# Twelve more homes for feed-forward tiles, output rows interleaved with tiles, and 159 instead of 153 key blocks on VectorE's exp

## Chip, core and metric

One core of one Trainium2 chip runs the kernel. The metric is the device time of one launch in microseconds (us). A change of 0.2% is about 1.4 us here.

## What is computed

The reference is a transformer block whose two branches run in parallel on the same normalised input, with B = 1, S = 2048 tokens, D = 512, 32 heads of 16, and a feed-forward width of F = 1792:

```python
xn = layernorm(x)
q, k, v = split_heads(xn @ wqkv)
p = softmax(q @ k.T / 4)
attn = (p @ v) @ wo
h = relu(xn @ W_gate) * (xn @ W_up)
return x + attn + h @ W_down
```

The softmax makes 32 x 2048 x 2048 exponentials, and they are what the kernel is built around.

## The kernel before

The queries are cut into four chunks of 512 (`c4`), the 32 heads into four groups of eight (`gg`), each in two halves (`ee`): 32 attention blocks in that order. A block runs over 16 key blocks of 128 keys (`kt`). One key block holds four scores tiles of 128 keys x 512 queries, one for each of four heads.

**TensorE works in two halves.** Nearly every matmul uses a 64x32 tile of the array, and four of them side by side make one *group*: 64 rows by 128 columns on 512 streamed columns. The upper and the lower 64 rows are two *halves* with a chain of groups each, and the two run side by side. `score` (L1289 and after), `pv_stream` and `mm_chain` all record such groups. A group is preceded by a load of its weights unless the half still holds them from the group before (`emit`, L389 to L396), which is how three value products over the same values can share one load.

**Two ways to take exp.** A usual key block is two *units*. A unit is two score groups (one on each half) into one of two double PSUM banks, then one ScalarE instruction of 128x1024 (L1365) that writes exp into `ring`, and later two value groups (`ring` by `v_aug`). As there are two such double banks, the scores of unit u+2 can't start before the exp of unit u has read its bank, and the exp of unit u+2 can't start before those scores are there. In a key block marked in `QUAD_AT`, `quad` does the work without ScalarE: four score groups into single banks, four VectorE instructions that turn each bank into 16-bit integers which are read as bf16 numbers (L1320), then two further patterns of the same integers shifted by constants, one by VectorE (L1339) and one by GpSimd in two pieces (L1335, digit 2 in the table), or otherwise divided. All three patterns go through the value product, so a marked key block has six value groups (24 matmuls of 64x32) where the two units of a usual one have two for the pair (8 matmuls); the scores take four groups either way.

**Background work.** Between the scores and value products TensorE also makes the feed-forward tiles (`glu`: 16 groups into two banks, then a VectorE copy L1016 and a VectorE product L1020 that leaves a 128x512 tile in `hT`), and the output rows (`out_rows`: 14 tiles by `W_down` and four attention outputs by `wo`, 36 groups into one bank, a VectorE addition L1069 and a store). Rows of a chunk can start only when its attention is done. `seq` lists tiles and rows in the order in which they are wanted: 14 tiles of a chunk (some made next to the same tile of the next chunk, so that one transfer of their weights from memory serves both), then that chunk's four rows; a loop below it gives each job its wanted unit. Finished tiles live in `hT`, 20 places (`NHS`, pool `P_h`).

**The order is written out.** The instruction order of all engines, with every bank and place, comes from the string `PLAN`, made beforehand by a planner that isn't in the file. `Graph.run` (L324) only decodes it and adds the waits; each engine then runs its queue strictly in that order. So a change of tables or of `seq` comes with another whole order. Names that the steps below use: `ring` (ScalarE's exp), `qd` (VectorE's), `v_aug` (values), `hT` and `xnT` (the normalised input, transposed, 4 x 2048 columns, which is dead once a chunk's last projection and tile have read it; at the end the last rows' residuals are kept in its first 1024 columns by `resid`).

Of the kernel before, what the change touches and what calls it, by code (L numbers as in the profile page):

```python
# [121 lines left out]
PLAN_OPS = 8248  # L122
PLAN = (
    "c-m!K1z;3M7v67n?{Wzd96~7)9Euky#fn1{v}hoK;8KbdcXx*Z#UWUc1S{?yij?ARg%p<nA>8f!Z)SJzHvEN<&E4+Ilka`+dvmFxr2dbKFK%6lf2^OxpPcvTGN*FSxG*2!#(Uzg@iI@fAXj{^<+x8@"
    "%6)Si-}BZZIh1?Wi;8boZof|$L0|XHm3{A9SJrLzy}8dF<9#T;*NnG~=Zyz+<6X!r<1XE12mQnqv4Rfy92EJAaiv>UfZpcj3mo26tqZQ$U$U%#_ciYGN&bQHBUf~J#l2=5&xoHaJB&+R@m)eUmxgY6"
    "1Mf<TVy*7=RX$=o=v_jrEyKoj@vvM?guuAZe1Kaql;**5!dTnG<bKeNI7+LmDA0wmjtHuEL0$U9ZE&$8Qryc8bEQY-YT!n=#1=+S<f4Xo@?W{UVg>|8pbR&RMXi6VU8KqKRjx=k#ie36ubayl(KlZZ"
    "Hkp@Zm}T5xJ)_w0XF*%xKB#iV=avr+x@m*ulCD_6H(%v;1K@*@uf*hc-3Kr$F6MW|ECM5~#yipxX1ho6K#?I4w=!QwxG%ZBoN;c4Gq+cx`6k)JEI2SPpBQc_9_EqpWxi+|cG5G(8XkzOFxxIx2)WG;"
    "v#>-|tRzVEh^;*em;WkE095*CSm<HqH|`M|cr09qT?N{VqVkBF%{%E!F2OyVSrjJo#C@^#5)-#ki(ELx!R42&{H1*&2Hxz52r$buahFFFHO%CC#9Q)JX4)?UB?Bn-@h~$EIv~rA8_Cs;WrYXK$Nit2"
    "M!^`XNhfIu!$pr-LS8yEID~)F1h<%6rs(#5!hPxRm9Y^lkGYG%5gr*R0~OLCGBU+!z=V64=^WYo$tfJMfyPTKzOG}v;bF$wOvcRc*~FY;Bv>(tiF*u~8(XJvKX15AfN<jhZuJo_&2ULV6kSIO6u07Z"
    "n^5&Yev|jYSj=N$RJvkR9J6dQw^K}4WnknQ2KJbTo4lwq%O)-%r<f?UuuDHk&%DjiSK&Se(yeb+R>Tduswg~lX?yeb(aF4Nkg+hqF8uHqwZ!ZoHmb)Pd?OPS5BUuDmX8s2!)cF~_zloVDiYqnivk~q"  # L130
    "nY1CwOy{3m@(zy-tptie8y<@zOv?m=nS1CyhNEu=B`7eOk-4-{f*<_M5>EDG7OrJlj3<qH<B}A0Uq6ShIT>w0_7VdV7WXDQb<H4KFK}%NhI8+iw?X?D-P<nA;$d8|bq!xzx2@%?Juea2d0J6Ycihz4"
    "iKpttb}qMXVl_42%G{@Q45=jhvlSWL=1(da;oV)g$rSi7X|g-_={ghMqMLJ*p}1~7rOW*c)nvS?_#*193-N&Jm2bY<vBgpM1wl8Rg-!aJs>hOTHhssvVvX}uy4D`TRBeJ=Dnik}C}X4+x2a?83x)z8"
    "P7M7D-$pVbhF-Mp(9NeUoO!Rm(9_&TEIgIe=U=4H*8F8n=~jp=p$ePY^|cgh5n-d%d3{m#82#JSWxiUqOr$1lsdSSV4fZs9w5f$mrt#t2l1_2~v;V<-Ua~WEtC}S<>(DK_7H`2Y3_dto2=#_e`(*Vt"
    "g9R+@W;o|D>5$AY83nqH+ATj!ijo4rE1_gF@^%OKB%gf8QYqHkoEu9rL-W|xonmNwAueE>v%JypMjKYVr8c%?2{)Cy)N9<j!4?E=hFLc`6E;RMR`D1WWsO<B25P)&-fH?P6*#ko0@_pi<kkdX=$0AY"
    "b-5+Vm{;o?c`)6VVKthH$2WqAMUB=5`+#hhw3ZGx!(`SvynFdD{aNE?a4o!<6(z;2ck1!(p?il87~_pKDf!TwTKRHY?HQuc1c<PXTbt^pKioTXnWmT_=C;>JnKGs*-f6>xf;lFcv!dN{GbE;9x6M>u"
    "tGxmi+^fa8t?L>ypru?bvh&uSabXVK-jem|O>Rzxu+2K$8f>l3FN?r5-n!Fl)?9I`7NeRin;X0Yo9|xdypb~dl5M=V+J(jQTxUwEcI)dZ+$){!Ga*kcp}qZ)f7yfok84w%BYZKC*;~J_!F>T9pD$Lg"
    "wKR=+qeb4{Dc*a8A$73TabdB#?_Tq~fZmp;6JjBm8p}iYu<YymJXI&NkD1(em|@|J+X7_G_r|e=PXlpp!?%=(#HU<JN3zp?4wWi>+}2KQ8>O0Xl~f(sUZ(aVEw7$1k1xLH;Kqe{xT0`h;%p~f+y@f="
    "#p_;p@l;sh|G&hSV$NGd7UwJG5s<F|7}p*}VZKms-w?tjWty|PhuKd*OpyhXdll~h=qn<#3DUrn>{8^QZP1{H!?fBMj-cq?QyE3E23c=Ev+<-S)iIUHH1ypZowzl}*=oWjam0RH`z&R)mpDwI*-m<l"
    "-F07|Ft;`PiA9;#$$+)7uNRn3de2=9BdmiRk7BV6Yy}`&q(#PxSMb=*&x}+UozfUkpjaJ1w?-jDoZ4;U)~S*uq%4Y&t;FXmw^OfTQ-I1BptV7t`zB_<CwadlFOM}``;H!TQ?!_AHAhZ!d{$sJG>=UO"
    "d1G(1JfA4^wjMd;d86r_>22g_Vaiy^I@dFhV5&6Ejjp4Z+@^aMF;t8<-d594yhLR-ck95_cb;iKjx_V)v%mzJUGsU*?d;;frr#{In(EdXI=L}cf7WRB=e`4Acp1*BBi%UrvQE+zZg1!O|IYQTpS{dx"  # L140
    "$|c2ys{fY|+}6kKyz0d?-RgE28MgEzPu+w6uRGfN0k;H!ZxG?BdGL$7?I$6yW7*dV?1#Dh3u@)c7oS1c(QXGk=cxuQ+j&6h-r^gM6#U;x*8FCdAKuy4dLFh;>zmGX?)#j=D_LNDBBJ|t@SUU^D|oNG"
    "M@eQ@eZ#68w``rwHXEfvi<LiPH*@+_yo0?-A76~WHm_}JMuA-z!_p~&aCK4lrdEM9=c{hTMrZa<ldK$CM^8M}NNqn`u~d7itaI<-d#ZGCdp^DL$d(S9+jf{4kHI>%GGj?J$jx(H&OFv==beibWBj$w"
    "78R@SS;vST>oWzj$$7kEnRwbf@3So{=Ky95OXf)@^Du9dvMExXS<|k0<X}IAlAVehW?Lud<{+jh7R`IfT(=$E8T`X+XIOfwdXXSEWS_y&1}vCIM1iOJ>_oTb3-hBKZYg`8#b$f-wtZ`&P<-0ME;qcN"
    "W?8gsJ#CF~)`xSjv$|!Ki4?1)n`5H)Lm1hi%mXT)q~c!=S2k+09pR?_e1xYyd9&$m`-j1)`nmT5Q!hmM7jusHsZ>W%itn>jbJnr5lwFbXR39v*5(Zx?Z`((whHU3H;p`pAQk}(k&-)al+T16Uzxcc&"
    "RfzZ(AKAh7nJ)KDNvYgVb!h87$m7PG<dye!D)1ho=wEzNXdB<`r}MtHl4=^TO)p;6<^2>uNeu~KRCV||_LpmkzZsDFzXwh@Kfi|x##s@lx~l4@OK6(^Csp@P!L#(5pL!pe@iZ&^#O;|ikDrJBIxmN5"
    "HyIw}rPmy8`iIeXaYL}@CCkXz)iBM;{=sc}|0W6mIT%9TF{GhwRDQm6LOGnKJ#hi`S>=^LuFA(Mvz@dGeWyQ22CA=YyP#~k7n$CqnbBT%{vHFAOSuPp9hmHNyRHGnpJhl1czXvZ@+yt?%5lBqEqc@K"
    "@_R-$`0WU;wk3kD(v2yNW0SWbxDXIBDo1;b7GB<w?bB-Q9d#?VO&GuTs1t4fJ`RoPZvgPB*F*%hUk^NU?IE`537o-SWpLtorXIj=Ps8zN+UJ=nlmRZTja;7+{Vi~5Y3r40x)<%XeXmzN98`{cN^-j0"
    "fu(`{F5Suacfe8S^3L<yulNl(wMc8P4gG2hurmG8JuJLbLm*xomQu&X;_m{dn{NBjHD;vVzeC}x6wC2>@8r@So!kn<J)Xg@6mqj))2D1m*$32$)E&z^YR$--<((F{UF=7%#r{*^W`WB^)n9=rxgPDQ"
    "F$@^z!spLh&jO=dZ*wFEJR1U(Y>?tmH#HqWacd6enr7=R0b|ywiw~4apw}i8|0^YJlC~U($=(JN-4uw6IC5O?5kC!R<Qj;_tJ^PH2Q(dosa@yM#i(sl`-DB99ZKc8l^^L6{ssoejoj}(hq;xHhVQ6^"
    "_5pg|S+BPP37FY?QgYyj1fXJ)BYg^Rfc%(<&jVNH1S(I%uS3T#j`HgrA#VMU2H#w!2$TX^6=9d%MP>qZS7G_}f_d(=7<26m(DGjP$!Okc4p1W4ec74QbrSd!{oSsj4VwVRdydASi3GN%(=P%CS<j0o"  # L150
    "qTL6w)EqZzLh0SQs^94KFA(XcPe$L*<VWkzepAqE7K&c}2FC}vV`HG6Am~QB%XaR1QsDYv?@RkPd<^>Ncj7jXv(%C@IFk`*=y)IU-v1AvKKx>v&Fn*oeTeSgM<OYN(9`)Ckl3u<!gZ}xk%K6#Vy#gU"
    "I1&1jn=L^UW&8*l)zuDGIZBsR9xyB!`rrEMp{s#r&*D(54m(AV>8qbYI$+wI?(-cnYbag$_xa&Tb2r(Mh;lKpQOjfIQSmve&VC$#`hSwjiNJwgJ5cBMN<iMFXup&%Kl%L-jQ<@d_z8Y*6AAG74x!Sm"
    "uL*G&F^+oEi2YR#CL$9D=Jv+qq2q^AEk6l-h#U`5n2O?7*0d=RJ0I+-yQgywAonsP^`ugKg3E1cj2+gZLqW=9w!GJztl_!Rny2R8gwsHUuP0-G`!3aI*um=Bvh5Q^S~t6!<HC*RC9@JVSsU(PwD@j("
    "p4)=6P-GbTC*70t$y20NHHuP~E{kIpclj6DAGf4<bSi<*UjhH&{PpCLDSkD9;aVrm?}o7Zi0g%{EjBh=*NVb_16iDp@UjqX@!wgOqUBdJ10$;3DEKyD;m?nFmfBQ~>|HBh9b**}7{a~*Hq6ooU}`_S"
    "Z$Z_Y2?v`#IpU(ro10o;Rg(>r-R(%xTMXj=u68THwj?KWJJDcUeQZwB)C{gFK+>Ojc6@f?M=G4MC%*MNx#caDTD$&J7hTozP|EK8MG$HdUnlS%;)Rq3o1BfdeD$bwe9jvM?jGanno|M@RON2gyaHuB"
    "eIkb@Y}|}Bt+AR#mdD|y1i`{crcznwI94O&kVb5B8)<h|z|pF2D+6=tr$Ov8igxAJXveA%ym0-m3g<pXlOH1*eB2!2^gmtv-QEfMsfwq1Q4A8wYbS^)#_N8qvIAv1()PCt^qYK@XL>gln3SUe)~8G-"
    "!(U=Ki$)C~YMs_t8&%*F@aPg&W$ZJ%M;_p8!r^5kU9PX`@d^R15|lsPk*gD5=%G~Y!pjU)QvdV;{;jpI>Or<;<}85Xe`}q);EjYGz>rQja)XNR^!y~3uB*EMfA&Kwtcc+?b3WME=2Losv3aLr5lwIX"
    "F!b4y(<4S_&)%6_x{e7IPnA6tPql=7wf6m0_C!T?Y`eIfkhkM$a5aL*mCg(3{caD&(Q88)5mRE-1GNs+fIqQE?MGTD5z)E#^j_d%zHw(lS0aZFY;i}|x@+!krTagpmbC({lLFS_2O#UZzs53GZ~xJw"
    "2UGr$;ef6c0}<5-<}QQBU4{gYEq0+*o`vZCp4_UHHWKSzb(@=ME%94d%r5YBGq4W}oXG)iT`7)D#9f0QW3FF{)?#DhZdCWqmY=A(^em048#3cXz5KvbN8yXbFY%05i1xPPZ1^6xL#JdEWDWD-(d*#o"
    "Fkp7_Q@t=c06+gZ2xAvv%REs^TXyW2<yr;IDCT~J%n^bZR%2R8cT{XEs+g!wSW+zvZ`Re~QNWI5?Ll_eUu7d>o7}w2L+Vlcob~fO=-r+Ip>uEE+`a(%mdMBn9T#ug;D@Wr>SJ4N!ogu2{Givz!5Oq("  # L160
    "ySIo>AvYtn;Fhas$(01ks_rFYwQWS#ZC!Y{>)Vk;lAl|x?24X4LU|*?=@z$NV|}Rb>%vvWi0X!xMnbV`NSZ3}{xWxs&6s|!beq_-h(9uV=JS7Z6Ov1}x$~yoFS98~#OC#av^6526Z=f5`R+`C=GStN"
    ">8GYeu5h%6yEU+6>re6Z<GVj}5Kew0Na9spdZ;PW*EfyZDGF^#WlzN=`6!bigT@Uigb;FS9LoPVxJ;8(mnu-0j^bp|pf`K+7QFs8g7IPn+*=Bbs_0K-da*Cj`08m<g|9CeGG>Sa$+X*wF8XqvzO$um"
    "m-=;cPsttb{0!zyUWMnqsZor(9X9wDbF@B3u-}Hof3#?ixP@KNb=>OhlSt!?bewF*V&Z^7NH@7Q1ta72MinsgS3Vsj<JRN)n|d!W0r-nGsLXTVQrKLeAHvtiKc+l5kJQ{(MTMSFM$dI=&?M-!NEETE"
    "{3vnmK;ifC8Sy_+wU(cP3Mc1KmT(^#W85c2&18r=Qgu3hCU-W5BFk_puWD_IqW4UMQsFkPyF_d5pXvD&^6pSI=v{xx#~H$jk|SB~rwlsr@%%<>_C<jxs@A4A)J8t7NBAz!JCYoao?+BTj3US<CSrKi"
    ">L5!Vt?iM-2-eS$lpM7@3(inN9wY^9SXY0f=wWS9^*+zu?&YQxK=(%4vgWIWJw5SkL&xSo&_u028%;tis6%D<hi)s6_d(}Ioq(GEcFH<(C;@y8Vw!AdLQ18j5;&`49kih}hj2F=pDB7T?b*H}nr-F>"
# [1252 lines left out]
```

## Time and profile before

| | us |
|---|---|
| median of the three runs | 685.31 |
| lowest and highest run | 685.06, 686.58 |
| span of the profiled execution, first to last instruction | 684.2 |

The page gives no device time of the profiled execution beside its span, so the 1.1 us between span and median is taken as what lies around the span. In the rows that follow, PE is TensorE's matmuls, PEld its weight loads, DVE VectorE, ACT ScalarE and POOL GpSimd; a "<-" after an idle time names who ended it. A row of the timeline merges instructions that follow each other: its first number is when the first one starts, its second how long until the last one ends, and x is their count.

### The profile page before, as it was taken

What the parts mean: (1) busy time and instruction counts of PE and PEld (TensorE: products, weight loads), DVE (VectorE), ACT (ScalarE), POOL (GpSimd) and SP (SyncE); (2) the same over time, 40 slices, a digit from 0 to 9 for tenths busy, and PEclk for the clock granted to TensorE, in tenths of its full rate; (3) what the DMA queues carried; (4) which work ended last, traced back from release to release, by engine and by line L of the source; (5) the groups of instructions that cost most, each with busy time, mean ns of one, the idle gap of its engine ahead of it and who ended that gap; (6) DMA issues with size and microseconds to landing.
All of it is one profiled execution on the core that took longest, in us unless ns stands there. A gap on an engine that the chain in (4) does not pass through costs nothing.

```text
span 684.2 us, 45020 instructions
## 1 busy us (share of the span) xinstructions
PE 675.6 (99%) x22262; PEld 345.9 (51%) x19654; DVE 598.5 (87%) x1012; ACT 666.8 (97%) x730; POOL 499.8 (73%) x507
## 2 busy tenths in 40 slices
...
DMA packets 55940, 35.86 MB, mean 52 GB/s; under 512 B 19336, under 2 KB 51784, under 8 KB 55752
## 3 DMA queue, kind: packets, MB, share of 16 engines
...
## 4 chain that ended last, share of the span: by engine, by line
PE 75%; ACT 18%; DVE 5%; issue 1%; DMA 0%; POOL 0%; ACTq 0%
PE ps L250 75%; ACT ring L1365 18%; DVE stats L726 1%; DVE qd L1320 1%; DVE xn_sb L739 1%; DVE v_aug L876 0%; DMA x_sb<-in_A_x_dram 0%; DVE qT L952 0%; DVE mv L727 0%; ACT xn_sb L1164 0%; DVE qd L1339 0%; DVE xnT L780 0%; POOL rstd L721 0%; DVE xnT L1075 0%; DVE kT L869 0%
## 5 line engine op out<-in xcount | busy, mean ns | idle before, releaser
L1365 ACT ACTIVATE ring<-ps 128x1024 bf16<-128x1024 f32 x718 | 660.4, 1141 | 2.9 <-PE ps L250 2.5
L1335 POOL TENSOR_TENSOR qd<-qd,ints 128x512 int32<-128x512 int32 x446 | 450.5, 1041 | 143.8 <-DVE qd L1339 73.2
L250 PE MATMUL ps<-qT,kT 64*32 64x512 bf16 x8192 | 448.7, 374 | 1.3 <-DVE qd L1320 0.4
L1320 DVE TENSOR_SCALAR qd<-ps 128x512 int16<-128x512 f32 x612 | 396.7, 685 | 51.9 <-PE ps L250 49.0
L250 PE MATMUL ps<-qd,v_aug 64*32 64x512 bf16 x3672 | 263.0, 375 | 1.1 <-issue 0.9
L250 PE MATMUL ps<-ring,v_aug 64*32 64x512 bf16 x2872 | 236.5, 374 | 0.1
L1300 PEld LDWEIGHTS <-kT 64*32 64x32 bf16 x7584 | 151.1, 92 | 126.6 <-issue 32.6
L1272 PEld LDWEIGHTS <-v_aug 64*32 64x32 bf16 x4544 | 108.7, 91 | 75.6 <-issue 20.4
L250 PE MATMUL ps<-xnT,wgs 64*32 64x512 bf16 x1792 | 137.6, 374 | 0.0
L250 PE MATMUL ps<-xnT,wus 64*32 64x512 bf16 x1792 | 136.4, 374 | 0.0
L250 PE MATMUL ps<-Wd,hT 64*32 64x512 bf16 x768 | 59.0, 375 | 0.0
L810 PEld LDWEIGHTS <-wgs 64*32 64x32 bf16 x1792 | 43.1, 91 | 31.5 <-issue 7.4
L810 PEld LDWEIGHTS <-wus 64*32 64x32 bf16 x1792 | 43.2, 91 | 29.8 <-issue 7.6
L1339 DVE TENSOR_SCALAR qd<-qd 128x2048 int16<-128x2048 int16 x83 | 56.1, 690 | 2.3 <-PE ps L250 2.2
L810 PEld LDWEIGHTS <-hT 64*32 64x32 bf16 x1792 | 40.2, 92 | 28.2 <-issue 4.2
L250 PE MATMUL ps<-Wv,hT 64*32 64x512 bf16 x512 | 45.7, 375 | 0.0
L250 PE MATMUL ps<-Wk,hT 64*32 64x512 bf16 x512 | 42.8, 375 | 0.4 <-DVE qd L1320 0.3
L1020 DVE SCALAR_TENSOR_TENSOR hT<-ps,up_sb 128x512 bf16<-128x512 f32 x56 | 38.4, 685 | 4.6 <-PE ps L250 4.2
L1016 DVE COPY up_sb<-ps 128x512 f32<-128x512 f32 x56 | 38.4, 685 | 3.1 <-PE ps L250 2.5
L250 PE MATMUL ps<-Wo_p,x_sb 64*32 64x512 bf16 x480 | 40.2, 374 | 0.6 <-issue 0.5
L250 PE MATMUL ps<-xnT,Wq 64*32 64x512 bf16 x480 | 36.2, 375 | 0.0
L250 PE MATMUL ps<-xnT,Wk 64*32 64x512 bf16 x480 | 35.0, 374 | 0.3 <-DVE xnT L780 0.3
...
## 6 DMA issues: line engine op xcount, KB each, us to landing
...
```

The costliest lines, as they stand in the source:

```text
L250: return e.add_instruction(mybir.InstMatmult(name=e.bass.get_next_instruction_name(), engine=mybir.EngineType.PE, ins=[e.lower_ap(x), e.lo ...
L726: G.op("DVE", 580, lambda e, m=m: e.bn_stats(stats[:, m, :], xs(m)), reads=[t_xm[m]], writes=[t_st], prio=pr, order=last_xn if m == 4 else ())
L739: G.op("DVE", 320, lambda e, m=m, t=t_n: e.tensor_scalar(xn_sb[:, t.slot, :], xs(m), mv[:, m, 0:1], rstd[:, m:m + 1], op0=ALU.subtract, op ...
L810: e.ldweights(w()[rows, 32 * j:32 * j + 32], tile_position=(rows.start, 32 * j))
L1016: G.op("DVE", 603, lambda e: e.tensor_copy(up_sb[:, tup.slot, :], bank_of(tu)), reads=[tu], writes=[tup], prio=-590)
L1020: G.op("DVE", 603, lambda e: e.scalar_tensor_tensor(out=hT[:, th.slot, :], in0=bank_of(tg), scalar=0.0, in1=up_sb[:, tup.slot, :], op0=ALU ...
L1272: e.ldweights(vs(j), tile_position=(64 * half, 32 * j))
L1300: e.ldweights(ks(m), tile_position=(64 * half, 32 * m))
L1320: G.op("DVE", 601, lambda e, j=j, tx=tx: e.tensor_scalar(qd[:, tq.slot, 512 * j:512 * j + 512], ps[:, BANK[tx.slot], :], IBIAS[3], 0.0, op ...
L1335: G.op("POOL", POOL_NS / POOL_PIECES + 60, lambda e, x=x, n=n, c=slice(i * m, i * m + m): e.tensor_tensor(x().bitcast(I32)[:, c], raw().bi ...
L1339: G.op("DVE", 600, lambda e, n=n, x=x: e.tensor_scalar(x(), raw(), float(SHIFTS[n + 1]), None, op0=ALU.add), reads=[ti, tq], writes=[t], p ...
L1365: exp_ops[u] = G.op("ACT", 904, lambda e, tr=tr, k0=k0: e.activation(ring[:, tr.slot, :, :], ps[:, 4 * k0:4 * k0 + 2, :], ACTF.Exp, scale= ...
```

## The change

It has three parts: the pool of finished tiles gets 12 places in `xnT` (four for each of the first three chunks, usable for tiles of later chunks), a chunk's four rows move behind `ROW_STEP` tiles each of the next chunk, and six more key blocks are marked in `QUAD_AT`, one in each of the attention blocks 10, 12, 18, 21, 26 and 28. `PLAN` is another string, with 8302 instead of 8248 entries.

```diff
+ROW_STEP = (0, 1, 2, 2)
...
-    "2...3..3..2..3..",
+    "2.2.3..3..2..3..",
...
-    "3...3..3..2..3..",
+    "3.2.3..3..2..3..",
...
-        P_h = Pool("h", NHS)
+        P_h = Pool("h", NHS + 12)
...
+        def h_of(t):
+            if t.slot < NHS:
+                return hT[:, t.slot, :]
+            a, dt = divmod(t.slot - NHS, 4)
+            return xnT[:, dt, 512 * a:512 * a + 512]
...
-            th = t_h[(c4, ft)] = Tile("h", P_h)
+            th = t_h[(c4, ft)] = Tile("h", P_h, list(range(NHS)) + [NHS + 4 * a + dt for a in range(c4) for dt in range(4)
+                                                               if c4 < NB - 1 or a == 2 or dt in TAIL_ACT])
...
-                out=hT[:, th.slot, :], in0=bank_of(tg), scalar=0.0, in1=up_sb[:, tup.slot, :], op0=ALU.max, op1=ALU.mult),
+                out=h_of(th), in0=bank_of(tg), scalar=0.0, in1=up_sb[:, tup.slot, :], op0=ALU.max, op1=ALU.mult),
...
-                    pairs.append(((lambda th=t_h[(c4, ft)]: hT[:, th.slot, 128 * i:128 * i + 128]), (lambda ft=ft: wd_of(ft))))
+                    pairs.append(((lambda th=t_h[(c4, ft)]: h_of(th)[:, 128 * i:128 * i + 128]), (lambda ft=ft: wd_of(ft))))
...
-                         reads=[t, txr], writes=[tr] + (t_xnT if i == 0 else []), prio=p1)
+                         reads=[t, txr], writes=[tr] + (t_xnT if i == 0 else []) + [Tile("res%d" % a, P_h, [NHS + 4 * a + i]) for a in range(2)], prio=p1)
+                resids.append(o)
...
-        seq = []
+        seq, behind = [], []
         for c4 in range(NB):
-            rows = []
+            rows, tiles = [], []
...
-                seq.append(ffn[ft])
+                tiles.append(ffn[ft])
                 if ft in shared[c4]:
-                    seq.append((0, GN, lambda s, c4=c4, ft=ft: glu(c4 + 1, ft, s), W_LEAD + 2))
-            seq += rows
+                    tiles.append((0, GN, lambda s, c4=c4, ft=ft: glu(c4 + 1, ft, s), W_LEAD + 2))
+            step = ROW_STEP[c4]
+            for n, row in enumerate(behind):
+                seq += tiles[n * step:n * step + step] + [row]
+            seq += tiles[len(behind) * step:]
+            behind = rows
+        seq += behind
...
+        for a in range(3):
+            guard = Tile("xnT")
+            guard.r.extend(o for o in t_xnT[a].w + t_xnT[a].r if o not in resids)
+            P_h.cur[NHS + 4 * a:NHS + 4 * a + 4] = [guard] * 4
```

More of the change, by code (lines that the diff above doesn't have):

```diff
@@ L77 @@
     "2...3..3..0..3..",
-    "2...3..3..2..3..",
+    "2.2.3..3..2..3..",
     "2...3..3..0..3..",
-    "2...3..3..2..3..",
+    "2.2.3..3..2..3..",
     "2...3..3..0..3..",
@@ L93 @@
     "2...3..3..0..3..",
-    "2...3..3..2..3..",
+    "2.2.3..3..2..3..",
     "2...3..3..0..3..",
-    "2...3..3..2..3..",
+    "2.2.3..3..2..3..",
     "2...3..3..0..3..",
@@ L119 @@
 NHS = 20
[L122 removed]
+PLAN_OPS = 8302
 PLAN = (
[L124 to L165, printed above, removed]
[L166 to L218 removed]
@@ new lines @@
+    "c-mcC2Ow4N`#;Y)_g<T_652zlv?Zj{l+r>;C244BP+HoQwx~!-qFpGFku;6=x3s6xP_!lPJ?H<9b1uJsxcA(1-t)fC_&m?^d7pD*nE(AJ;6Fh+!Y|S%{L}I+I&8_jr3c~-0=<TR>1pAACKQ<Zb1mMXKjxjdO#S`R"
+    "E##WGTK%d*!*K$d1pU3Iq6z9H>V*&*3dPW)`T;y6fWZI1fxx350be2KKoXmrWTYeVNkA8QGz5J_KjaXN<^dlGcpfxa{pviOnkR=0J-}k4bE06P8a!EBeTobf>Q^Vn<Q~ylJQ12)z%Sy`SUOR1A^^TdhZDI#5b8Cc"
+    "Isi|tK;$Q*#ij9mqV!aIvOGB?>jJ(^43E!{8|dA{c0@K18n{3Zqys7ih}a^AMAB1b$=q00EEIJL8bse1(cyw<2_RRb6{XWeYPF5YB0RMeh<BlnEM7~6uhBtt9_kfF2~-sP!c#O*U6Gz@De;Qb9t@UUTt!@o*pN=f"
@@ new lines @@
+    "tL-R?Cb?9agb^A*TLP<EWeN<sq-c4v1k0#EtuV0_))$|p4kLzCflwc1;wqvK$n<qGY8^71r9vRn5Fypl5_hmFR>g?s;RP}T-B2%^Mh#kx73T+PJAz^nTmrQuqlTCmVk*%?jEY)WAU>eNh|);zBZ$Q6k(=;8e2+>1"
+    "^un-Aee`4b#1N8#3j`HQk%uN=Yh`#8uax1%kY?1XR3406q^)E@bTc)K3Sk0Gf<KUnk+v$9c$OvW5!vxfJWGwK!Y;=XsK`|;A~iNO7%Mp%B-e;Az;=}UMc#RyuBrk??Je>FucS60F|3NF7a}W-Kc1+Lr2r9g3^th<"
+    "7-()B{w(&57<A+$i-%K*iHs_OE78b;O27v-3gUb!q8RER;#dqwbv|Hd&JjenQzfXHcs8;Mky79Z(9jtb^$VJj=uLznXF)6l$SS;AcL{BPJjB!}NP@w5B#ThYQO}WOh&seaEFO=>(I`@hp^kru7({hJ#fdtJ@kr7r"
@@ new lines @@
+    "HW?bjk%Wxz=OwG+NySy@irBC~6;dOWXpKhjJS&bvi<8>~>S}61sADNGuuX{VS%zYatbn6}r71xCOb_vNwHgB81pt4f83|8Sqe(48j8Z47QLq$ryzoy`ov#IT;gj;9<Y@S-5LhY)F%EVTQH+`lxkpUB47IgNbQ^I7"
+    "LsbS|gc5_1B#po`Qd3}`5VaU3N3P-|Kua$UK;jY+KjI2%SL1mYh9y%Fn-SquKtqLuCkC&WeMz9=+e9xAUy&?|wILZ!prI$alo*p|STTSpS_!V`Xp~O{o(3rvnYu<rOCd=kL~$e>s3@>`MyfsNtddO0NRa16xT#aT"
+    "nkexqP6{(}0qU~{#SK+PsON6zwOX5LKsRWL=6Oy!K`WwY$_A_o`9S!8m5CNNkrOlo2!5%Rt5Y5?h{#muVYHqgU8Z9gb%McvWGzCpRIJ2=Xqr>vkOlD`n$g6xsbVMwNJdrh>>nK!l8hzkSF92YrA90{rd|=L2QM*A"
```

152 lines of the change are left out of this document (97 added, 55 removed).

## The prediction

> **What bounds the kernel now.** I read the page's totals first, then ScalarE's timeline over the whole span, then TensorE's timeline in a dense spot, and last the order in which the groups stand in the two programs' TensorE queues.
>
> ```profile
> PE 675.6 (99%) x22262; PEld 345.9 (51%) x19654; DVE 598.5 (87%) x1012; ACT 666.8 (97%) x730; POOL 499.8 (73%) x507
> ```
>
> Two engines are nearly full. TensorE's 99% is a modelled share, so it has to be weighed otherwise. ScalarE's timeline is firmer:
>
> ```profile
> 10.91 2.87 ACT L1365 ACTIVATE ring<-ps 128x1024 bf16<-128x1024 f32 x3
> 14.10 146.19 ACT L1365 ACTIVATE ring<-ps 128x1024 bf16<-128x1024 f32 x159 [0.32 <-PE ps L250]
> 160.47 2.85 ACT L1365 ACTIVATE ring<-ps 128x1024 bf16<-128x1024 f32 x3 [0.17 <-PE ps L250]
> 163.63 22.10 ACT L1365 ACTIVATE ring<-ps 128x1024 bf16<-128x1024 f32 x24 [0.31 <-PE ps L250]
> 186.10 38.83 ACT L1365 ACTIVATE ring<-ps 128x1024 bf16<-128x1024 f32 x42 [0.37 <-PE ps L250]
> 225.36 182.36 ACT L1365 ACTIVATE ring<-ps 128x1024 bf16<-128x1024 f32 x198 [0.42 <-PE ps L250]
> 408.64 265.61 ACT L1365 ACTIVATE ring<-ps 128x1024 bf16<-128x1024 f32 x289 [0.92 <-PE ps L250]
> 680.25 0.60 ACT L1164 ACTIVATE xn_sb<-ps 128x512 bf16<-128x512 f32 x1 [6.00 <-PE ps L250]
> ```
>
> The 718 exps run from 10.91 to 674.25 (408.64 + 265.61): 663.3 us, 0.924 each, with six gaps that TensorE ended. How fast they can follow each other shows in a calm stretch, and in the view of their line:
>
> ```profile
> 125.36 20.27 ACT L1365 ACTIVATE ring<-ps 128x1024 bf16<-128x1024 f32 x22
> ```
>
> ```profile
> L1365 ACT ACTIVATE ring<-ps x718: 1017/1146/1314, 10.9 to 673.1; 128x1024 bf16<-128x1024 f32 x180
> ```
>
> With 1.02 to 1.31 for the last exp alone, the 21 steps before it take 18.96 to 19.25 us, 0.903 to 0.917 each. I take 0.904 as the floor and 0.91 as the usual step. Over the floor the 718 lose some 14 us (663.3 less 718 x 0.904). So ScalarE sets the pace, and TensorE takes a little from it.
>
> How near is TensorE?
>
> ```profile
> 160.76 0.38 PE L250 MATMUL ps<-xnT,wus 64*32 64x512 bf16 x4
> ...
> 160.86 0.38 PE L250 MATMUL ps<-xnT,wgs 64*32 64x512 bf16 x4
> ...
> 160.97 0.38 PE L250 MATMUL ps<-xnT,wus 64*32 64x512 bf16 x4
> 160.97 0.10 PEld L810 LDWEIGHTS <-wus 64*32 64x32 bf16 x4
> 161.08 0.38 PE L250 MATMUL ps<-xnT,wgs 64*32 64x512 bf16 x4
> ...
> 161.19 0.38 PE L250 MATMUL ps<-xnT,wus 64*32 64x512 bf16 x4
> 161.19 0.10 PEld L810 LDWEIGHTS <-wus 64*32 64x32 bf16 x4
> ...
> 161.40 0.38 PE L250 MATMUL ps<-xnT,wus 64*32 64x512 bf16 x4
> ```
>
> The groups of `wus` on one half start at 160.76, 160.97, 161.19 and 161.40, 0.215 apart, while the other half runs `wgs`. The queue of before holds 2768 groups on each half: 595 us, 0.829 for each exp, 92% of the floor. An exp's step has room for 4.2 groups, but groups come whole: with four between one unit's scores and the next unit's TensorE is early, with five it is 0.171 late (1.075 less 0.904), which only the slack of the two score banks can absorb.
>
> **The change, part by part.** The rows that price its operations:
>
> ```profile
> L1335 POOL TENSOR_TENSOR qd<-qd,ints 128x512 int32<-128x512 int32 x446 | 450.5, 1041 | 143.8 <-DVE qd L1339 73.2
> ...
> L1320 DVE TENSOR_SCALAR qd<-ps 128x512 int16<-128x512 f32 x612 | 396.7, 685 | 51.9 <-PE ps L250 49.0
> L250 PE MATMUL ps<-qd,v_aug 64*32 64x512 bf16 x3672 | 263.0, 375 | 1.1 <-issue 0.9
> L250 PE MATMUL ps<-ring,v_aug 64*32 64x512 bf16 x2872 | 236.5, 374 | 0.1
> ...
> L1339 DVE TENSOR_SCALAR qd<-qd 128x2048 int16<-128x2048 int16 x83 | 56.1, 690 | 2.3 <-PE ps L250 2.2
> ```
>
> *ScalarE:* six key blocks lose two exps each, 12 x 0.91 = 10.9 us less on the engine that sets the pace. *TensorE:* a marked block has 24 value matmuls (3672/153), a usual one 8 (2872/359), so 96 more, 12 groups on each half, 2.6 us. That makes 2780 groups for 706 exps, 0.847 each, 94% of the floor: the mean still fits. *GpSimd:* 12 pieces at 1.01 are 12.1 us into 143.8 us of idle time, nothing. *VectorE:* 24 conversions at 0.648 (396.7/612) and six patterns at 0.676 (56.1/83), 19.6 us. Its cover, stage by stage (the third busy time is VectorE's):
>
> ```profile
> 200.00:250.00 50.00, 49.72 (x1672) 27.70 (x1464) 42.52 (x71) 49.52 (x55) 40.42 (x41) 1.00 0.15 41
> 250.00:300.00 50.00, 49.67 (x1704) 25.61 (x1508) 44.07 (x72) 49.81 (x55) 42.84 (x43) 1.00 0.22 62
> 300.00:350.00 50.00, 50.00 (x1656) 23.49 (x1420) 47.88 (x81) 50.00 (x56) 36.80 (x37) 1.00 0.16 44
> ```
>
> A marked block costs VectorE 3.3 us; blocks 10 and 12 lie in the first two stretches, with 7.5 and 5.9 us idle: 0 on the path. With that cover gone TensorE waits for banks, at most the 19.6 us, which I leave to a rival.
>
> *Homes and rows:* 11 of the 56 tiles go to `xnT`, the same VectorE instruction to another address: 0. Their new waits name matmuls far ahead in the queue; held up behind such an instruction would be conversions, and TensorE behind those, but a chunk is dead long before. The rows' 12 loads of `x` and 12 stores keep their number; on SP's queue the transfers of q and of the sums stand behind them as before, so 0 for these too. What the interleaving does change is where TensorE's groups stand, and that is the large term.
>
> *Weight loads:* 5461 groups load weights, where 4884 did, since the three patterns of a key block seldom follow each other on a half now. In the rows above a load of 0.10 stands inside each step of 0.215, so 0.
>
> *The order between the scores:* in each program's queue I counted, on the fuller half, the groups from one unit's scores to the next unit's. Before: five 104 times, six once. After: five 219 times, six 18 times, seven 7 times, eight once, and three or fewer 93 times in the place of 41. Over ten successive units (from the 20th on) before never has more than 42 groups (9.03 us, just what ten steps of 0.904 take); after has 43 to 47 in 86 places, 85 of them in units 238 to 309, 408 to 462 and 569 to 620, where rows and tiles alternate. In units 238 to 309 one half has 305 groups, 65.6 us, for 72 exps that want 65.1. Before has 286 there (61.5 us), in a stretch where ScalarE was hardly idle:
>
> ```profile
> 231.50:298.50 67.00, 66.67 (x2304) 34.90 (x2028) 58.01 (x95) 66.81 (x74) 56.28 (x56) 1.00 0.19 53
> ```
>
> The price: I carry a half's lateness on from unit to unit at 0.215 a group and 0.904 an exp, never below zero. If the banks absorb nothing, ScalarE loses 18.0 us before and 49.1 after, 31.1 more. If they always absorb 0.171, one five, it is 0.8 and 12.7, 11.9 more. Both ends have rows. The 22 exps from 125.36 hold one five and lost nothing; the gap at 160.47 follows a six right behind a five, the one at 163.63 two fives in a row. So single fives are mostly absorbed and runs are lost, and the after order is full of runs: nearer the lower end, 16 us.
>
> *The tail:*
>
> ```profile
> 673.46 6.77 PE ps L250 x204
> ```
>
> Behind the last scores stand 33 and 34 groups where there were 29 and 31, and ScalarE's 6.00 us wait at 680.25 says that the end waits for them: three groups, 0.6 us.
>
> **The sum:** -10.9 + 16 + 0.6 = 5.7 us on a span of 684.2, which gives 689.9. The median of the runs lies 1.1 above that span, so 691.0. With 11.9 and 31.1 for the jams it would be 686.9 and 706.
>
> **The rivals.**
>
> *A, faster: ScalarE's count alone decides.* The score banks and the lighter units (93 of three or fewer) swallow the jams, and the exps go on at the pace of before. For it speaks that the mean, 0.847, is under 0.904 and that 42 groups in ten units cost nothing. Against it: 47 groups in ten units are 10.1 us, more than any bank can hide. Time: 685.3 - 10.9 + 0.6 = 675.0. It decides as soon as fewer than 10 us of the jams reach ScalarE. [...]
>
> *B, a wash.* Jams of 10 to 11 us just eat the gain: 685.3, within 1.4 us.
>
> *C, VectorE becomes the bound.* Between 300 and 350 it is at 47.88 of 50. If rows and conversions bunch in its queue, TensorE's scores wait for the single banks: half of the 19.6 us on top of the forecast's sum, 701. Against it, TensorE waited for VectorE hardly anywhere before, and VectorE itself waited 49.0 us for TensorE at L1320.
>
> *D, weight loads show.* 577 more loads at 0.095, shared by two halves, are 27 us: at worst 718, half of that 704. The rows above speak against it. [...]
>
> **How the numbers follow.** Forecast (jams of over 12 us): 0.54. A, gains of over 1.4 us, whole or in part: 0.24. B: 0.10. C: 0.08. D: 0.04. Within 0.2%, 1.4 us, is about what a measurement of this kernel can't tell from no change: same 0.10, faster 0.24, slower 0.66. The likeliest case alone reaches from 687 to 700, or 706 at its upper bound. The range goes down to 677, near A's full gain, and up to 702, past C's 701.
>
> **What would show it.** In the after profile: 706 exps, with idle time of ScalarE that TensorE ended well over the 2.5 us of before and most of it around 230 to 305, 390 to 440 and 540 to 590 us; a mean step near 0.947 ((663.3 - 10.9 + 16)/706); VectorE's line of conversions at 636 with its idle time before them still ended by TensorE; `wus` groups still 0.215 apart with their loads. Wrong would be: a mean step at or under 0.925 (rival A), TensorE's idle time ended by VectorE's conversions in those stretches (C), or steps of 0.3 between groups of one half that wait for nothing (D).

## The result, and the profile after

| | before | after |
|---|---|---|
| median of 20 runs each, side by side, us | 685.28 | 686.85 |
| lowest and highest | 684.0, 686.87 | 684.75, 688.54 |
| span of the profiled execution, us | 684.2 | 685.9 |

The ratio is 1.002 (95% interval 1.0012 to 1.0028): 1.6 us slower, just past what can be told from no change. The forecast was 691.0.

The page of the changed kernel: busy totals, the queue of instruction packets, and two groups (busy, mean ns, idle time before them and who ended it):

```profile
PE 677.1 (99%) x22355; PEld 382.0 (56%) x21962; DVE 619.1 (90%) x1042; ACT 661.2 (96%) x718; POOL 511.4 (75%) x519
...
q8 instruction: 173, 2.83, 1.6%
...
L1389 ACT ACTIVATE ring<-ps 128x1024 bf16<-128x1024 f32 x706 | 655.0, 1058 | 9.4 <-PE ps L260 7.5
...
L1344 DVE TENSOR_SCALAR qd<-ps 128x512 int16<-128x512 f32 x636 | 413.4, 685 | 34.8 <-PE ps L260 30.5
```

The rows of the page of before that answer to the second and third:

```profile
q8 instruction: 164, 2.69, 1.6%
...
L1365 ACT ACTIVATE ring<-ps 128x1024 bf16<-128x1024 f32 x718 | 660.4, 1141 | 2.9 <-PE ps L250 2.5
```

The 12 exps are gone, and ScalarE now waits 7.5 us for TensorE in place of 2.5. VectorE's conversions still wait for TensorE (30.5 us), and no row of TensorE's own waits names them at 0.3 us or more. A smaller row will matter: 173 packets of instructions instead of 164. Where ScalarE waits shows in its timeline (start, length, count, idle time before it):

```profile
11.45 17.84 ACT L1389 ACTIVATE ring<-ps 128x1024 bf16<-128x1024 f32 x19
...
162.01 69.19 ACT L1389 ACTIVATE ring<-ps 128x1024 bf16<-128x1024 f32 x75 [0.26 <-PE ps L260]
231.39 2.86 ACT L1389 ACTIVATE ring<-ps 128x1024 bf16<-128x1024 f32 x3 [0.19 <-PE ps L260]
234.90 12.67 ACT L1389 ACTIVATE ring<-ps 128x1024 bf16<-128x1024 f32 x13 [0.66 <-PE ps L260]
248.04 1.94 ACT L1389 ACTIVATE ring<-ps 128x1024 bf16<-128x1024 f32 x2 [0.47 <-PE ps L260]
...
256.50 15.18 ACT L1389 ACTIVATE ring<-ps 128x1024 bf16<-128x1024 f32 x16 [0.62 <-PE ps L260]
...
308.62 101.79 ACT L1389 ACTIVATE ring<-ps 128x1024 bf16<-128x1024 f32 x110 [0.43 <-PE ps L260]
...
608.91 65.58 ACT L1389 ACTIVATE ring<-ps 128x1024 bf16<-128x1024 f32 x71 [0.33 <-PE ps L260]
674.83 1.02 ACT L1389 ACTIVATE ring<-ps 128x1024 bf16<-128x1024 f32 x1 [0.34 <-PE ps L260]
```

There are 24 gaps ended by TensorE where there were six, and most lie at 231 to 309, 410 to 462 and 555 to 609 us, the stretches in which rows and tiles alternate. So the place was forecast rightly. The mean step is 0.941 (675.85 less 11.45, over 706), close to the forecast's 0.947 and above rival A's sign of 0.925. I add up every step from one exp's start to the next above 0.904: before 14.0 us over 717 steps, after 26.1 over 705. The difference of the spans then closes: 12 exps at 0.904 are -10.9, the gaps +12.1, the first exp starts 0.5 later (11.45 for 10.91), and the end changes by 0.1 or less: +1.7.

The question for the experiments is what the 12.1 us are made of. Below, T and O stand for the forecast's theory (the order: over-full runs of groups between scores), D for rival D (weight loads show), C for rival C (VectorE), and F for a theory that came out of the first batch: TensorE's instructions are not supplied in time.

### The profile page after: what moved, and what is told of

Its sections match the earlier page's. It is cut to its first block, busy times and chain, and to the rows that moved or that the text cites. A ratio compares the mean times of both kernels' runs of the same rounds, so it can differ in the third digit from the quotient of the medians.

```text
span 685.9 us, 47477 instructions
## 1 busy us (share of the span) xinstructions
PE 677.1 (99%) x22355; PEld 382.0 (56%) x21962; DVE 619.1 (90%) x1042; ACT 661.2 (96%) x718; POOL 511.4 (75%) x519
## 4 chain that ended last, share of the span: by engine, by line
PE 91%; DVE 6%; ACT 2%; issue 1%
PE ps L260 90%; DVE qd L1344 3%; ACT ring L1389 2%; PE ps L918 1%; DVE qd L1363 1%; DVE stats L736 0%; DVE xn_sb L749 0%; DVE v_aug L886 0%; PE ps L1404 0%; DVE xnT L790 0%; DVE up_sb L1034 0%; DVE hT L1038 0%; ACT xnT L782 0%; DVE xnT L1038 0%; DVE o_sb L1222 0%
## 5 line engine op out<-in xcount | busy, mean ns | idle before, releaser
L1359 POOL TENSOR_TENSOR qd<-qd,ints 128x512 int32<-128x512 int32 x458 | 462.2, 1039 | 136.3 <-DVE qd L1363 72.8
L260 PE MATMUL ps<-qT,kT 64*32 64x512 bf16 x8192 | 471.8, 374 | 2.3 <-issue 1.0
L1344 DVE TENSOR_SCALAR qd<-ps 128x512 int16<-128x512 f32 x636 | 413.4, 685 | 34.8 <-PE ps L260 30.5
L260 PE MATMUL ps<-qd,v_aug 64*32 64x512 bf16 x3816 | 316.0, 375 | 0.3
L260 PE MATMUL ps<-ring,v_aug 64*32 64x512 bf16 x2824 | 246.6, 375 | 0.0
L1324 PEld LDWEIGHTS <-kT 64*32 64x32 bf16 x8052 | 166.0, 92 | 108.8 <-issue 18.8
L1296 PEld LDWEIGHTS <-v_aug 64*32 64x32 bf16 x6384 | 154.3, 92 | 85.6 <-issue 15.6
L1363 DVE TENSOR_SCALAR qd<-qd 128x2048 int16<-128x2048 int16 x89 | 63.2, 718 | 0.5 <-PE ps L260 0.3
L260 PE MATMUL ps<-Wv,xnT 64*32 64x512 bf16 x576 | 38.1, 374 | 0.0
L260 PE MATMUL ps<-Wk,hT 64*32 64x512 bf16 x384 | 36.1, 375 | 0.0
```

The costliest lines, as they stand in the source:

```text
L260: return e.add_instruction(mybir.InstMatmult(name=e.bass.get_next_instruction_name(), engine=mybir.EngineType.PE, ins=[e.lower_ap(x), e.lo ...
L1296: e.ldweights(vs(j), tile_position=(64 * half, 32 * j))
L1324: e.ldweights(ks(m), tile_position=(64 * half, 32 * m))
L1344: G.op("DVE", 601, lambda e, j=j, tx=tx: e.tensor_scalar(qd[:, tq.slot, 512 * j:512 * j + 512], ps[:, BANK[tx.slot], :], IBIAS[3], 0.0, op ...
L1359: G.op("POOL", POOL_NS / POOL_PIECES + 60, lambda e, x=x, n=n, c=slice(i * m, i * m + m): e.tensor_tensor(x().bitcast(I32)[:, c], raw().bi ...
L1363: G.op("DVE", 600, lambda e, n=n, x=x: e.tensor_scalar(x(), raw(), float(SHIFTS[n + 1]), None, op0=ALU.add), reads=[ti, tq], writes=[t], p ...
```

## Experiments

Each kernel was timed in rounds beside the kernel before on the same chip; ratios are to that, with 95% intervals. The changed kernel's own ratio is the 1.002 above, from another chip than most, so a difference of 0.1% between two kernels is not read.

### Loads, and fewer columns in the output rows

The kernel before, every group loading its weights; order, matmuls and results stay:

```diff
-            elif held[o.half] == o.wkey:
+            elif False:
```

> The kernel before, with every TensorE group loading its weights: 652 group loads more, the order of groups unchanged. Theory T (the gain of 12 exps is given back because groups stand in over-full runs between the units' scores): no change, 685.3 within 1.4 us. Rival D (the 577 more weight loads of the changed kernel are what gave the gain back): the 12.0 us that ScalarE lost more there, times 652/577, 13.6 us, so near 699.

Measured: 700.41 us beside a before of 687.9, ratio 1.0181 (1.0138 to 1.0225). Loads cost 12.5 us here, near D's 13.6; T's no change missed. How they cost shows in TensorE's timeline around one of ScalarE's gaps:

```profile
595.31 0.38 PE L250 MATMUL ps<-xnT,wus 64*32 64x512 bf16 x4
...
595.52 0.38 PE L250 MATMUL ps<-xnT,wgs 64*32 64x512 bf16 x4
595.53 0.49 PE L250 MATMUL ps<-ring,v_aug 64*32 64x512 bf16 x4
595.74 0.38 PE L250 MATMUL ps<-xnT,wus 64*32 64x512 bf16 x1
595.74 0.49 PE L250 MATMUL ps<-qd,v_aug 64*32 64x512 bf16 x4
597.32 0.38 PE L250 MATMUL ps<-xnT,wus 64*32 64x512 bf16 x3 [1.08 <-issue]
```

The steps on a half are still 0.21 with a load in each. But at 595.74 one group stops after the first of its four matmuls, and both halves stand until 597.32, waiting for nothing that the profile shows ("issue"). A group has no wait between its four matmuls, so I looked at the instructions themselves. I numbered TensorE's instructions in queue order and listed the places where neighbours inside one group start over 60 ns apart ("breaks"): 19 before, 165 after, 383 here. All 23 breaks over 0.3 us here, and all ten after, are at one place of every 256 instructions, number 76. The 652 added loads of four instructions are 2608, ten times 256, and the page's packets go from 164 to 174. The pages count 41916 matmuls and weight loads for 164 packets before and 44317 for 173 after, 256 to a packet. So I read a packet of 16 KB (2.85 MB/174) as a block of 256 of TensorE's instructions. The traces of before, of the changed kernel and of this run give the times: the next block's packet starts a median 0.8 to 1.1 us after the block before has begun, takes about 1.0, and no block began less than 1.17 us after its packet had landed; the 33 that broke a group for over 0.3 us, here and after, began 1.19 to 1.59 us after it. My estimate from these three (the wait for the packet's start, its length, and the 1.17) is some 3.2 us from one block's start to the earliest start of the next, and 3.9 for a late one (the 95th percentile), while two halves that load in each 0.215 step use 16 instructions in it and a block in 3.44 us.

Most breaks are not at that place: 335 of the 383 here and 145 of the 165 after are 60 to 204 ns long and lie elsewhere in a block, 265 and 130 of them within 2 us behind a break at its start. So most of them follow a break at a block's start; what makes them no run isolates.

The other two take three quarters of the columns off the row chains of the first three chunks, to make the places with rows light (`rows_a` from the changed kernel, `rows_b` from before):

```diff
-            mm_chain(t, pairs, reads, pr, slots=slots, sub=sub)
+            mm_chain(t, pairs, reads, pr, slots=slots, sub=sub, cols=128 if c4 < NB - 1 else 512)
```

> The changed kernel with the same rows on 128 of their 512 columns. Theory T: with TensorE's runs broken the 12 exps pay in full, so it lies 8 to 11 us under the kernel before with short rows, at 663 to 672. Rivals C (VectorE) and D (weight loads): it stays within 2 us of the kernel before with short rows, or above it, since neither of these is touched.

> The kernel before with the output rows of the first three chunks computed on 128 of their 512 columns only (the other columns are left out): 216 groups a half stream 128 columns, some 33 us less on TensorE, ScalarE, VectorE and the order unchanged. Theory T: only what TensorE takes from ScalarE's 14 us goes away, so 673 to 681.

Measured: `rows_a` 694.01, ratio 1.0103 (1.0062 to 1.0144); `rows_b` 685.38, 0.9971 (0.9954 to 0.9988). T fell badly here, with 663 to 672 and 673 to 681 expected: with less work on TensorE the changed kernel became slower, with 271 breaks for 165, and `rows_b` gained 2 us with 122 for 19. That `rows_a` stays above `rows_b` is what C and D expected.

### Another order

Five kernels move groups in TensorE's queue and leave the rest of the work alone. `lev_a` puts each score group earlier where groups had piled up ahead of it; `lev2_a` moves a unit's two scores together; `skiplev_a` is `lev2_a` with the skipped loads of the next section; `ord_a` and `ord_b` have another order of all filling groups. The edit of the first three is a reordering of `queue["PE"]` behind `run` (shown for the second and third; `lev_a` has its own `level`, called with 0.0), that of the last two another `PLAN`, with 33 loads fewer in `ord_a` and 258 more in `ord_b`:

```diff
         G.run()
+        G.level(171)
```

> The changed kernel with the same work, but in TensorE's queue the scores of a unit stand earlier wherever more groups than one exp's step holds stood ahead of them (five or more between two units: 148 times where it was 245; lateness carried on with nothing absorbed 27.6 us where it was 49.1, with one five absorbed 6.2 where it was 12.7; six groups more at the tail, 1.3 us). Theory T: ScalarE gets back 6 to 12 us less the 1.3, so 676 to 682. Rival C (VectorE's 19.6 us more are the bound) and rival D (weight loads): 686.9, or 688 with the tail.

> The changed kernel, in which both score groups of a unit move earlier in TensorE's queue, together, where more than a group's length beyond 0.904 us of groups had piled up ahead of them (0.171 us). Units that leave more than 0.171 us of lateness fall from a sum of 12.7 us to 1.1 us in the groups' count; the number of loads is as it was (5468). T, the jams: up to 11 us come back, 676 to 682. F, the supply of instructions alone: no change, 686 to 688.

> Both at once: the scores moved earlier, and no loads for the value groups of the second and third pattern of marked key blocks (4880 loads; the same part left out). If jams and supply both had a share, this is the lowest of the three, 673 to 678, the 675.0 of ScalarE's count alone within reach. If one of them was all of it, it equals the better of the two.

> The changed kernel with TensorE's groups in another order: nothing is added, left out or taken to another engine, and the loads are as many (5428 for 5461). Groups that fill the spaces between scores were moved by up to some tens of places, so that fewer of them stand ahead of a late pair of scores, and so that two groups of opposite halves that add into the same bank of PSUM stand further apart. O, the order of the groups made what is left of the 12 us after the loads' 3.5: 5 to 10 us come back, 677 to 682. V, something that the order doesn't touch (VectorE, the supply of instructions): 685 to 688.

> The kernel before with its groups put into another order in the same way (5142 loads for 4884, 258 more). O: the order of before left less to win, and the loads cost some of it (258 at 6 to 19 ns are 1.5 to 5 us): 681 to 687. If it wins as much as the other, the order of the change was no worse than that of before.

Measured ratios: `lev_a` 1.1222 (1.1193 to 1.125), `lev2_a` 1.0458 (1.0431 to 1.0485), `skiplev_a` 1.0364 (1.0345 to 1.0384), `ord_a` 1.0214 (1.0195 to 1.0233), `ord_b` 1.0164 (1.0148 to 1.0181). All slower, none as any theory had it. For `lev_a`, 84 us slower, the view of waits (total, count, longest) says a part of why:

```profile
PE ps L260 <- ACT ring L1439: 33.4, 55, 1.2
```

TensorE stood idle for 33.4 us in 55 waits that an exp ended: scores stand so early there that their bank is still being read. The count of groups between scores that I forecast from has no such term. Whether halves that came out of alternation, or groups of opposite halves closer together on one bank, had a part is not shown. In `lev2_a` that row is 7.8 us of 31, and in the two with another `PLAN` it is 0.4 or less, so for these the cause is open. The five say that none of these orders betters the one given by `PLAN`, and nothing about the 12.1 us. The one clean reading is `skiplev_a` against `lev2_a`: the same 588 loads fewer are worth 0.9%.

### Fewer loads, order untouched

```diff
+            elif o in self.noload:
+                o.load, o.wsrc = False, ()
...
+                if t is not ti:
+                    G.noload.update(G.ops[second:])
```

> The changed kernel, in which the value groups of the second and third pattern of a marked key block load no weights and multiply by what their half of TensorE holds (the sum over keys of these patterns is thereby left out; every matmul, every exp and the whole order of the four queues stay). 4879 groups then load weights in place of 5461, as few as in the kernel before (4884). T, the jams alone: the order is untouched, so 686.9, within 1. F, TensorE's instructions come in too late: with 580 group loads fewer some 2300 instructions leave the queue; of 12.0 us that ScalarE lost more than before, the part that stalls of supply made (estimate 4 to 8 us) goes: 679 to 683. If F made all of it: 675 to 676.

> The kernel before with the same loads left out: 114 group loads fewer (4770 in place of 4884), order untouched, the same part of the computation left out. F: a gain of 0.5 to 3 us, 682 to 685, as the kernel before has few places at which instructions come late. T: no change, 685.3 within 1.

Measured: `skip_a` 685.3 beside a before of 687.41, ratio 0.9971 (0.9959 to 0.9983); `skip_b` 0.9987 (0.9975 to 0.9998). Against the changed kernel's 1.002 that is 0.5%, 3.5 us, just short of the 4 to 8 that F expected; T expected nothing. Breaks fall from 165 to 61, packets to 164:

```profile
q8 instruction: 164, 2.69, 1.7%
...
L1395 ACT ACTIVATE ring<-ps 128x1024 bf16<-128x1024 f32 x706 | 654.0, 1057 | 8.3 <-PE ps L260 6.6
```

What such a stop does in the changed kernel itself shows at its gap at 248.04:

```profile
246.57 0.38 PE L260 MATMUL ps<-Wd,hT 64*32 64x512 bf16 x4
246.61 0.38 PE L260 MATMUL ps<-Wo_p,x_sb 64*32 64x512 bf16 x4
246.79 0.42 PE L260 MATMUL ps<-qT,kT 64*32 64x512 bf16 x6
247.63 0.37 PE L260 MATMUL ps<-qT,kT 64*32 64x512 bf16 x2 [0.42 <-issue]
247.64 0.38 PE L260 MATMUL ps<-qd,v_aug 64*32 64x512 bf16 x2
```

The scores of a unit (two groups, eight matmuls) stop after six, and the last two, with which a block begins, come at 247.63, 1.50 us after that block's packet had landed. I would have put this gap down to a full run. Behind the first 20 exps, after has 39 steps over 1.1 us from exp to exp, 13.8 us above the floor together; a break of over 0.1 us stands beside 15 of them, with 5.3 us. In `skip_a` it is 5 of 32, with 1.5 us. The difference, 3.8 us, is close to the 3.5 of the times, though a break beside a step need not have made it. All steps together fall by 2.2 only (26.1 to 23.9). The profiled execution of `skip_a` has one stop of TensorE of 1.6 us, before 329.96, that also ends at the first instruction of a block; that block's packet had landed 4 us before, so this stop is not explained.

### VectorE, and the full runs themselves

`vec_a` shortens VectorE's first operation, `thin_a` takes 45 groups out of the 26 over-full places, `thinc_a` takes as many out elsewhere:

```diff
+            cut = 128 if made_q >= 24 else 0
-                    qd[:, tq.slot, 512 * j:512 * j + 512], ps[:, BANK[tx.slot], :], IBIAS[3], 0.0, op0=ALU.add, op1=ALU.max),
+                    qd[:, tq.slot, 512 * j:512 * j + 512 - cut], ps[:, BANK[tx.slot], :512 - cut], IBIAS[3], 0.0, op0=ALU.add, op1=ALU.max),
```

```diff
         G.run()
+        G.thin(True)
...
+                    left = len(at[h][u]) - 5
+                    for o in at[h][u]:
+                        if left > 0 and free(o):
+                            gone[o] = True
```

> The changed kernel, in which VectorE's first operation on a score bank (the exp as an integer) works on 384 of the 512 columns, from the 25th marked key block on; the last 128 columns keep what an earlier block left (their exps are left out). VectorE's 540 such operations get about a quarter shorter, some 70 us of its 619 in all; TensorE, ScalarE and all orders stay. C, VectorE sets the pace of the six added blocks: at least 5 us faster, below 682. O and F, the order and the loads on TensorE: 685 to 687, as VectorE's 30.5 us of waits on TensorE only get longer.

> The changed kernel without 45 of its 5560 groups: in the 26 places in which six to eight groups of one half stand between two scores, all above five are left out (24 projection or feed-forward groups, 21 value groups; their products are missing from the sums). The order of the rest and all other engines stay. O, these runs cost what the trace of the changed kernel shows in them, 6.5 us beyond before: 5 to 8 us faster than the changed kernel, 679 to 682 beside a before of 685.3 (ratio 0.991 to 0.995). If the order is not it: 0 to 1 us (the 46 loads that go with the groups are 0.3 to 0.9 us).

> The control: the changed kernel without 45 groups too, but taken from places with four groups between two scores and four or fewer in the places beside them, spread over the whole run (their products are missing from the sums). As many instructions and loads fewer as in the run before this one; the 26 runs of six to eight stay. O: no change or as much as 45 loads are worth, 0 to 1 us (686 to 687, ratio 1.000 to 1.002). If the sheer number of groups counts (TensorE full on the whole): as much faster as the other.

Measured: `vec_a` 1.0094 (1.0068 to 1.0121), `thin_a` 1.009 (1.0075 to 1.0105), `thinc_a` 1.006 (1.0037 to 1.0083). All three took work away and became slower than the changed kernel's 1.002. The breaks: 333, 238 and 117. (`thinc_a` varies most, from 686.7 to 694.0 us; its profile is of an execution of 688.6.) By themselves they would clear VectorE and the full runs of any guilt, but in the first two the supply of instructions may stand in front of both. So the same again with the loads left out:

> The changed kernel without the 45 groups of the full places and without the loads of the second and third pattern's value groups (4841 loads, both parts left out). If order and supply of instructions are two causes that add: 3 to 4 us below the run without the 45 groups, 675 to 679 (ratio 0.986 to 0.991), close to the 675.0 that ScalarE's count alone would give. If they share one stall: no lower than the better of the two alone.

> The changed kernel with VectorE's shorter operations (384 of 512 columns from the 25th marked key block on) and without the loads of the second and third pattern's value groups (4879 loads). With the shorter operations alone the kernel was 0.7% slower than the changed one, and its instruction packets came later. F, that slowdown is the supply of instructions: with 580 loads fewer it goes, 680 to 684 (ratio 0.992 to 0.998), no slower than without the loads alone. If the shorter operations themselves disturb the order: it stays, 688 to 691.

Measured: `thinskip_a` 0.9958 (0.9943 to 0.9972), 32 breaks; `vecskip_a` 0.9935 (0.9921 to 0.9948), 50 breaks. The same loads (582, or 574 with the thinned runs) that were worth 0.5% in the changed kernel are worth 1.6% (10.9 us) beside a shorter VectorE and 1.3% (9.1 us) with the thinned runs. ScalarE's row in the pages of `vec_a` and of `vecskip_a`:

```profile
L1391 ACT ACTIVATE ring<-ps 128x1024 bf16<-128x1024 f32 x706 | 655.8, 1067 | 13.7 <-PE ps L260 11.6
```

```profile
L1397 ACT ACTIVATE ring<-ps 128x1024 bf16<-128x1024 f32 x706 | 652.3, 1078 | 6.0 <-PE ps L260 5.0
```

11.6 us of waits become 5.0 with nothing changed but loads. And with the loads out VectorE does count: 2.5 us against `skip_a`, intervals apart. The last three ask how far that goes (`vec2skip_a` has `cut = 256`):

> The changed kernel without the loads of the second and third pattern's value groups, and with VectorE's first operation on 256 of 512 columns from the 25th marked key block on (half of those exps left out; 384 columns gave ratio 0.9935 with the same loads left out, 512 columns 0.9971). C, VectorE sets some of the pace once instructions come in time: another 2 to 5 us less, ratio 0.986 to 0.991. If VectorE was out of the way at 384 columns already: no further gain, 0.992 to 0.995.

> The kernel before with the same two things left out: the second and third pattern's loads, and VectorE's first operation on 384 of 512 columns from the 25th marked key block on. Without the loads alone it had ratio 0.9987. C, the six added key blocks made VectorE a bound: here VectorE has 20 us less to do, so less comes back than the changed kernel's 2.5 us, 0 to 1.5 us (ratio 0.9965 to 0.999). If a shorter VectorE helps both kernels as much (2 to 3 us, 0.994 to 0.996), the added blocks are not what it shows.

> The changed kernel with all three: loads of the second and third pattern's value groups left out, VectorE's first operation on 384 of 512 columns, and the 45 groups of the full places left out. Loads alone gave 0.9971, loads and VectorE 0.9935, loads and groups 0.9958. If the full runs cost time that VectorE hid: 3 to 6 us below loads and VectorE, 0.985 to 0.989. If the full runs are worth only what they were, about 1 us: 0.991 to 0.993.

Measured: `vec2skip_a` 0.9947 (0.9933 to 0.9961), no further gain, so VectorE's part ends at about 2.5 us; `vecskip_b` 0.9978 (0.9967 to 0.999), 0.6 us under `skip_b` and within its interval; `vecthinskip_a` 679.85, 0.9897 (0.9881 to 0.9914), 2.6 us under `vecskip_a`, intervals apart, where thinning had given an unresolved 0.9 without the shorter VectorE. The control, as many groups out of calm places, was not run with the loads out, so whether it is the full places or any 45 groups that gave this is not shown. Its row:

```profile
L1467 ACT ACTIVATE ring<-ps 128x1024 bf16<-128x1024 f32 x706 | 651.8, 1078 | 4.0 <-PE ps L260 3.2
```

The runs that tell the causes apart, side by side:

| kernel | ratio to before | group loads | breaks | steps over 0.904, sum in us |
|---|---|---|---|---|
| before | 1 | 4884 | 19 | 14.0 |
| `skip_b` | 0.9987 | 4770 | 79 | 14.2 |
| `vecskip_b` | 0.9978 | 4770 | 93 | 15.7 |
| `loads_b` | 1.0181 | 5536 | 383 | 26.6 |
| after | 1.002 | 5461 | 165 | 26.1 |
| `vec_a` | 1.0094 | 5461 | 333 | 31.2 |
| `thin_a` | 1.009 | 5415 | 238 | 30.9 |
| `thinc_a` | 1.006 | 5418 | 117 | 27.2 |
| `skip_a` | 0.9971 | 4879 | 61 | 23.9 |
| `thinskip_a` | 0.9958 | 4841 | 32 | 21.8 |
| `vecskip_a` | 0.9935 | 4879 | 50 | 20.0 |
| `vecthinskip_a` | 0.9897 | 4841 | 48 | 17.4 |

Breaks and sums are of one profiled execution each. Breaks don't give the time by themselves (`thinc_a` has fewer than after): for 44 of after's 165 neither the step from exp to exp in which they fall nor the next one is over 0.92 us.

## Why the prediction was wrong in size

The sum had -10.9 + 16 + 0.6 = 5.7 us, and the spans differ by 1.7. The step that failed, and made the forecast too high, is the price of the jams: 16 us, where all gaps together grew by 12.1. A second step was wrong in its mechanism, the weight loads: put at 0, and worth 3.5 of these 12.1. So 8.6 us at most are left for what the 16 stood for. The one term was too high by 7.4 or more, the other too low by 3.5, and so they partly cancel.

*ScalarE, -10.9: right.* 12 exps at 0.904.

*Weight loads, 0: the step whose reason failed.* The argument was that a load of 0.10 stands inside each step of 0.215, and the steps are so, even where every group loads (`loads_b`). But the load is also four instructions, TensorE's instructions came in 173 packets in place of 164, and all ten breaks of over 0.3 us after stand at the start of a block. The prediction had the count, 5461 for 4884, and stopped at the 0.10. Where the loads were added, the view of weight loads shows. Before:

```profile
L1300 PEld LDWEIGHTS <-kT 64*32 64x32 bf16 x7584 | 151.1, 92 | 126.6 <-issue 32.6 <-DVE kT L869 1.4 <-DVE vare L719 0.7
L1272 PEld LDWEIGHTS <-v_aug 64*32 64x32 bf16 x4544 | 108.7, 91 | 75.6 <-issue 20.4 <-DVE v_aug L876 0.4
```

After:

```profile
L1324 PEld LDWEIGHTS <-kT 64*32 64x32 bf16 x8052 | 166.0, 92 | 108.8 <-issue 18.8 <-DVE kT L879 1.0 <-DVE vare L729 0.7
L1296 PEld LDWEIGHTS <-v_aug 64*32 64x32 bf16 x6384 | 154.3, 92 | 85.6 <-issue 15.6 <-DVE v_aug L886 0.4 <-DVE qT L962 0.2
```

1840 value loads more, 460 groups' worth, are four fifths of the growth. They lie in the second and third patterns of the marked key blocks: leaving their loads out takes 582 off after (5461 less 4879) and 114 off before (4884 less 4770). It cost 3.5 us in the changed kernel as it stands. What the 10.9 and 9.1 us beside a shorter VectorE and thinned runs have beyond that is mostly what those two kernels had lost against the changed one (1.0094 and 1.009 for 1.002, some 5 us each). Rival D was right that loads show; its mechanism (steps of 0.3; they stay at 0.21 in `loads_b` too) and its price of 27 us, or half of it, were not.

*Jams, 16: the term that was mis-sized, and only partly jams.* The gaps grew by 12.1, at the forecast's places and near its lower bound of 11.9, but that closeness is luck: 3.5 of it are loads. What the 26 places with six groups or more cost is 0.9 (unresolved) to 2.6 us as far as 45 groups left out tell it, without a control; what the fives cost by themselves no run isolates. By the trace alone I would have said more: the 26 steps with six groups or over are 6.8 us above the floor after and 0.3 before, and the steps with five 10.7 for 6.9, 10.3 of the 12.1 in all. Thinned to five, the same places still cost nearly as much (`thinskip_a`: 14.7 us on fives and none on sixes, `skip_a`: 8.9 and 6.3). So a count of groups between scores finds the tight places, but doesn't price them.

*VectorE, 0: off by about 2 us.* The cover was idle time by stretch, and it did not cover all: a shorter VectorE is worth 2.5 us with the loads out, 0.6 in the kernel before. By which wait, the views don't settle: TensorE's waits for the conversions are 0.4 us in `skip_a`, yet in the chain that ended last the conversions have 4% of the span there and under 0.5% in `vecskip_a`. Rival C had the engine and a price of 10.

*Tail, 0.6: 0.1.* From the last exp's end to the end of the span it is 10.05 us for 9.95. *Start:* the 0.5 us was not foreseen.

Rival A's condition, fewer than 10 us of gaps, did not come about; B's 10 to 11 was the nearest, its 685.3 within 1.4 us just missed. Loads, VectorE and thinned runs together take the changed kernel's gaps from 26.1 to 17.4 us and its ratio from 1.002 to 0.9897, 8.6 us. The 3.4 us that then still stand above the 14.0 of before stay without a cause that was shown. Why shorter work elsewhere brings more breaks at the same count of loads (165 to 333 in `vec_a`) also stays open, and so does `thinc_a`, slower than the changed kernel with fewer breaks.
